# A third row maximum per loop iteration that two heads share, in half-width matmuls, with the loop's transfers on SyncE

## The chip, the cores and the metric

The kernel runs on one core of a Trainium2 chip. Its engines work side by side, each through its own instruction queue in program order: PE (matmuls, and PEld for the weight loads that run ahead of them), DVE (vector work), ACT (activations), POOL (GpSimd) and SP (SyncE, which only issues transfers here). Matmuls write to PSUM, which has 8 banks of 512 float32 for each of 128 partitions. The metric is the device time of one execution in microseconds (us); less is better.

## The reference

The program computes a gated mix of two blocks on the same tokens x (2048 tokens, 640 features). Only block A, attention with 32 heads of width 20, concerns the change:

```python
scores = jnp.einsum("bhqd,bhkd->bhqk", q, k) * (Dh ** -0.5)
p = _softmax(scores, axis=-1)
o = jnp.einsum("bhqk,bhkd->bhqd", p, v)
a = o.transpose(0, 2, 1, 3).reshape(B, S, D) @ wo
```

Block B is a token-mixing MLP (layer norm, two matrices over the token axis, a gelu), and the result is g * a + (1 - g) * b with a sigmoid gate g for each token. Everything is float32.

## The kernel before

**Stages.** First the queries, keys and values are projected (to about 220 us). Then the MLP runs (to about 700 us). Then comes the attention loop (to about 1762 us), and last the output projection. What concerns us is the attention loop, lines 672 to 719.

**Two kinds of score tiles.** Heads are taken in pairs: head j of a pair (j = 0 or 1) keeps its keys and queries in the rows 64 j and up of a 128-row tile, so its matmuls use one half of PE's rows, and a matmul of the other head can run beside it in the other half. A softmax needs the maximum over all keys of each query ahead of the exponentials, so every score is computed twice.

- The *maximum tiles* (line 178, tile `s`): 128 queries against 512 keys of one head, a bank of 128x512 scores; `tensor_reduce` on DVE (line 180) takes the maximum over the 512 keys. A pair of heads has 128 such tiles: two halves of the queries, 8 blocks of 128 queries in each, 4 times 512 keys, 2 heads. After 64 of them `s_max` takes the maximum over the four blocks of keys (line 143, DVE), three small operations on POOL negate it and split it in two parts (lines 144 and 145), and 8 tiles later `s_store` transposes it (line 150, DVE), and it goes to DRAM (line 151). From there `load_m` brings it into two further rows of the queries' tile.
- The *exponential tiles* (line 700, tile `st`): the transposed scores, 128 keys against 512 queries, whose two further rows subtract the maximum; ACT exponentiates each from PSUM into `p` (line 703).

**One iteration.** The loop has 16 pairs times 32 iterations. An iteration takes one block of 128 keys (`kt`) against one half of the queries (`qh`): four exponential tiles (two heads, two times 512 queries), and then, in `pv_flush`, four matmuls side by side in PE's columns that multiply the *previous* iteration's exponentials with the values (line 637, tile `pv`; each shows as two rows in the profile, since plain float32 goes through PE in several passes). After 16 blocks of keys `pv_evac` copies the sums out (line 618, DVE) and stores them with 8 transfers on POOL's queue (lines 624 and 625).

**How the maximum tiles are spread.** 736 of the 2048 maximum tiles (`S_AHEAD`) are computed in the MLP stage. The other 1312 go into the loop, evenly: `due` (line 706) says how many there should be, and `take` of an iteration is 2 or 3 until they are given out, 28 iterations before the end, and then 0. With three, the order on PE is exponential tile, maximum tile, exponential tile, maximum tile, exponential tile, maximum tile, exponential tile. The halves of the rows alternate so that each maximum tile stands beside an exponential tile in the other half; the seventh matmul has nothing beside it. With fewer than three, one exponential tile takes a bank of the maximum tiles (`s_tile` in line 709).

**Banks.** The exponential tiles have four banks in turn (`st_tile`), the maximum tiles three (`s_tile`), and `pv` one. PE must wait for ACT or DVE to have read a bank before it writes there again.

**Queues.** PE's, ACT's and DVE's orders are those of the program; from the MLP on POOL's and SP's are too. On POOL's queue in the loop are the maxima's three operations, the maxima's store, the stores of `pv_evac`, the normalisers' loads and stores (`norm_steps`), and the load and split of the output weights (`load_wo`, with pairs 8 to 12). SP's queue has loads alone: `base_stack` of the next pair (keys and queries for the exponential tiles, 20 transfers, issued at iteration 6), `load_v` (at 12), `s_stack` (keys and queries for the maximum tiles, 18 transfers, at 14), `load_m` (4 transfers, at 27 for the next pair's first half and at 11 for the pair's second half).

Of the kernel before, what the change touches and what calls it, by code (L numbers as in the profile page):

```python
# [13 lines left out]
P = 128  # L14
# [14 lines left out]
def gated_mix(ctx, tc, xT, x, wqk, wv0, wv1, wo, w1, w1t, b1, w2, b2, out):  # L29
# [38 lines left out]
    def st_tile(shape, name):  # L68
        return psum.tile(shape, F32, tag="st", bufs=4, name=name)

    def s_tile(shape, name):
        return psum.tile(shape, F32, tag="s", bufs=3, name=name)

    def k8(shape, dt, name):
        return base.tile(shape, dt, tag="k8", bufs=3, name=name)
# [59 lines left out]
        c0 = NPAIR * (p % 8)  # L135
        nc.sync.dma_start(v_tiles[p], v_d[p // 8, :, :, c0: c0 + NPAIR].rearrange("t p c -> p t c"))

    s_close = []

    def s_max(p, half, mx):  # L140
        mm = cp.tile([P, 16], F32, tag="mm", bufs=2, name=f"mm{p}_{half}")
        mc = cp.tile([P, 32], F32R, tag="mc", bufs=2, name=f"mc{p}_{half}")
        nc.vector.tensor_reduce(mm, mx.rearrange("p k j t -> p (j t) k"), axis=AX.X, op=OP.max)
        nc.gpsimd.tensor_scalar_mul(mm, mm, -1.0)
        hi_lo(mc[:, :16], mc[:, 16:], mm, hi_eng=nc.gpsimd, lo_eng=nc.gpsimd)
        s_close.append([8, lambda: s_store(p, half, mc)])
# [5 lines left out]

    M_LAG = [8]

    def s_next():
        next(stream)()
        for e in list(s_close):
            e[0] -= 1
            if e[0] <= 0:
                s_close.remove(e)  # L160
                e[1]()

    def s_finish():
        next(stream, None)
        while s_close:
            s_close.pop(0)[1]()

    def s_tiles(p):
        for half in range(2):
            mx = cp.tile([P, 4, 2, 8], F32, tag="mx", bufs=2, name=f"mx{p}_{half}")  # L170
            for t in range(8):
                for kc in range(4):
                    for j in (1, 0):
                        def f(j=j, kc=kc, t=t):
                            ks, qs = s_src[p]
                            ps = s_tile([P, 512], f"s{p}_{half}_{t}_{j}_{kc}")
                            r = slice(64 * j, 64 * j + 3 * DH)
                            nc.tensor.matmul(ps, qs[half][r, t * P:(t + 1) * P], ks[r, kc * 512:(kc + 1) * 512],  # L178
                                             start=True, stop=True)
                            nc.vector.tensor_reduce(mx[:, kc, j, t: t + 1], ps, axis=AX.X, op=OP.max)  # L180
                        yield f
            s_close.append([2, lambda p=p, half=half, mx=mx: s_max(p, half, mx)])

    def s_stream(on_start):
        for p in range(NP):
            on_start(p)
            yield from s_tiles(p)

    hooks = [None]
    m_queue = [nc.gpsimd]  # L190
    stream = s_stream(lambda p: hooks[0](p))

    p1s = ExitStack()
    p1 = p1s.enter_context(tc.tile_pool(name="p1", bufs=1, side="right"))
# [353 lines left out]
    for n, _ in enumerate(steps):  # L548
        settle()
        while done + 2 <= S_AHEAD and done < S_AHEAD * (n + 1) / STEPS:  # L550
            if done == 48:
                s_src[1] = base_stack(1, False, None)
            if done == 4 * 128 + 40:
                st_src[0] = base_stack(0, True, None)
                for half in range(2):
                    load_m(0, st_src[0][1], half, lambda *a: drip.append(lambda: nc.sync.dma_start(*a)))
                drip.append(lambda: load_v(0))
            if drip and done % 4 == 0:
                drip.pop(0)()
            for _ in range(2):  # L560
                s_next()
            done += 2
    settle(True)
    while done < S_AHEAD:
        s_next()
        done += 1
    gps.close()
    hps.close()

# [14 lines left out]

    hooks[0] = start_loop
    M_LAG[0] = 0
    s_src[6] = s_stack(6)

    def norm_steps(h0, h1):
        b = (h1 - h0) * S // P  # L590
        a = S // b
        rl = ap.tile([P, 256], F32, tag="rl", bufs=1, name=f"rl{h0}")

        def load():
            nc.gpsimd.dma_start(rl[:, :b], l_d[h0:h1].rearrange("h (a b) -> (h a) b", b=b))

        def recip(i):
            nc.vector.reciprocal(rl[:, i: i + 64], rl[:, i: i + 64])

        def store(h):  # L600
            src = rl[a * (h - h0): a * (h - h0 + 1), :b]
            nc.gpsimd.dma_start(r_d[h].rearrange("d (a b) -> a d b", b=b), src.unsqueeze(1).broadcast_to([a, DH, b]))
# [13 lines left out]
    def pv_evac(p, qh, pv):  # L616
        ev = ap.tile([P, 512], F32, tag="oev", bufs=2, name=f"oev{p}_{qh}")
        nc.vector.tensor_copy(ev, pv)  # L618
        for j in range(2):
            h = 2 * p + j  # L620
            for c in range(2):
                r = 32 * (2 * j + c) + 11 * j
                cols = slice(qh * 1024 + c * 512, qh * 1024 + (c + 1) * 512)
                nc.gpsimd.dma_start(o_d[DH * h: DH * h + DH, cols], ev[r: r + DH, :])  # L624
# [19 lines left out]

    def load_wo(c):
        raw = ap.tile([P, D], F32, tag="wor", bufs=1, name=f"wor{c}")
        nc.gpsimd.dma_start(raw, wo[c * P:(c + 1) * P, :])
# [19 lines left out]
    def o_late(q):  # L667
        return o_part(q, slice((NC - 1) * P, D), 1, 512, "l", 4, nc.scalar, nc.vector)[0]

    turn = given = 0  # L670
    LEFT = NP * 128 - S_AHEAD
    for p in range(NP):
        ks, qs = st_src[p]
# [2 lines left out]
        for it in range(32):  # L676
# [20 lines left out]
            def st_op(j, c, tile):  # L697
                r = slice(64 * j, 64 * j + 3 * DH + 2)
                ps = tile([P, 512], f"st{p}_{it}_{j}{c}")
                nc.tensor.matmul(ps, ks[r, kt * P:(kt + 1) * P], qs[qh][r, c * 512:(c + 1) * 512],  # L700
                                 start=True, stop=True)
                pt = lp.tile([P, 512], F32, tag="pt", bufs=12, name=f"p{p}_{it}_{j}{c}")
                nc.scalar.activation(pt, ps, AF.Exp, scale=SCALE)  # L703
                pts[j, c] = pt

            due = min((p * 32 + it + 1) * LEFT // (NP * 32 - 28) + 1, LEFT)
            take = min(due - given, 3)
            for n in range(4):
                st_op((n + turn) % 2, n // 2, s_tile if n == 2 and take < 3 else st_tile)
                if n < take:  # L710
                    s_next()
            given += take
            if take and given == LEFT:
                s_finish()
            turn = (turn + take) % 2
            pv_flush()
            if p * 32 + it in later:
                later.pop(p * 32 + it)()
# [79 lines left out]
```

## Time and profile before

| | us |
|---|---|
| median of 3 runs (1843.85 to 1847.97) | 1845.69 |
| the profiled execution | 1846.6 |
| its span | 1844.8 |

The profiled execution is one run with the hardware profiler; its own time is 0.9 us over the median, and 1.8 us of it lie outside its span. PE's granted clock was 0.996 of full speed. In the loop (800 to 1700 us) the profile counts 1732 exponentials on ACT and 1175 maxima on DVE.

How to read it: a row of the timeline gives the start, the duration, the engine, the line, and how many instructions were merged. A weight load's start (PEld) marks the moment when PE gets to a matmul; its matmul streams behind it. The duration of a row holds the time to fill and drain the pipeline as well, so rows of one engine overlap, and the distance between starts is the rate. In square brackets stands how long the engine had been idle and what ended that, as far as semaphores tell.

### The profile page before, as it was taken

The page shows a single profiled execution, that of the slowest core. Times are in us where ns is not written, and L with a number is a line of the kernel's source. Part 1 is how long each engine was busy: PE and PEld are TensorE (multiplying, and loading weights), DVE is VectorE, ACT ScalarE, POOL GpSimd, SP SyncE. Part 2 cuts the span into 40 slices and gives each one's busy share as a digit, 9 for nine tenths or more (in the row PEclk, how much of TensorE's full clock was granted, in tenths as well). Part 3 has the DMA queues.
Part 4 walks back from the last instruction along what each step waited for, and adds up shares of the span by engine and source line. Part 5 has one row for each costly group of instructions (what it writes and reads, how often), then busy time and mean ns, then how long its engine had stood idle before and what let it go on. Part 6 is the DMA issues. An engine that isn't in the chain of part 4 may idle for free. (4 is left out here: it accounts for less than half of the span.)

```text
span 1844.8 us, 39129 instructions
## 1 busy us (share of the span) xinstructions
PE 1829.7 (99%) x14978; PEld 1135.2 (62%) x14978; DVE 1428.9 (77%) x2341; ACT 1361.6 (74%) x2688; POOL 637.1 (35%) x900
## 2 busy tenths in 40 slices
PE   9999999999999999999999999999999999999998
PEld 7998799999999994333333333333333333333378
DVE  4202299999999998888888888888888888888137
ACT  4243244465444448999999999999999999999930
POOL 1013478888887770112112111121321211212210
PEclk9999999999999999999999999999999999999999
DMA  8456766566645645504032324213540423301463
GB/s 289 143 169 212 222 173 173 158 194 193 168 139 166 189 136 121 118 15 103 20 85 61 73 42 93 57 50 78 107 103 24 109 47 77 71 14 23 131 219 132
DMA packets 152831, 216.61 MB, mean 117 GB/s; under 512 B 65698, under 2 KB 92082, under 8 KB 148738
## 3 DMA queue, kind: packets, MB, share of 16 engines
q1 hardware_dynamic: 129172, 178.68, 35.4%
q0 software_dynamic: 14688, 20.78, 5.2%
q10 hardware_dynamic: 8784, 14.65, 2.4%
q8 instruction: 118, 1.93, 0.4%
q14 instruction: 69, 0.57, 0.1%
HBM read 165.43 MB, written 48.25 MB: 116 GB/s over the span
## 5 line engine op out<-in xcount | busy, mean ns | idle before, releaser
L180 DVE TENSOR_REDUCE mx<-s 128x1 f32<-128x512 f32 x2048 | 1293.7, 684 | 159.9 <-PE s L178 119.7
L703 ACT ACTIVATE p<-st 128x512 f32<-128x512 f32 x2048 | 1042.1, 615 | 20.9 <-PE s L178 2.2
L700 PEld LDWEIGHTS st<-qs_True,ks_True 62*128 62x128 f32 x2048 | 307.3, 185 | 485.1 <-ACT p L703 312.9
L700 PE MATMUL st<-qs_True,ks_True 62*128 62x512 f32 x2048 | 579.6, 425 | 0.2 <-ACT ty L477 0.2
L637 PE MATMUL pv<-p,v 128*32 128x512 f32 x4096 | 555.5, 605 | 0.2
L178 PE MATMUL s<-sk,sq 60*128 60x512 f32 x1280 | 423.1, 434 | 0.0
L41 POOL TENSOR_TENSOR wl<-wr,wh 128x512 fp32r<-128x512 f32 x228 | 273.6, 1216 | 59.8 <-ACT wh L38 30.9
L624 POOL DMA_DIRECT2D o_d<-oev x128 | 67.0, 524 | 494.3 <-DVE oev L618 491.6
L178 PE MATMUL s<-ks_False,qs_False 60*128 60x512 f32 x768 | 225.1, 397 | 0.4 <-DVE mx L180 0.3
L46 PE MATMUL y<-gh,wh 64*128 64x320 f32 x896 | 216.8, 308 | 0.0
L46 PE MATMUL y<-gl,wh 64*128 64x320 f32 x832 | 210.3, 306 | 0.0
L46 PE MATMUL y<-gh,wl 64*128 64x320 f32 x832 | 209.4, 305 | 0.0
L38 ACT ACTIVATE wh<-wr 128x512 fp32r<-128x512 f32 (+2 forms) x246 | 135.9, 594 | 90.2 <-PE s L178 29.0
L178 PEld LDWEIGHTS s<-sk,sq 60*128 60x128 f32 x1280 | 197.7, 185 | 1.2
L637 PEld LDWEIGHTS pv<-p,v 128*32 128x32 f32 x4096 | 84.9, 108 | 171.4 <-issue 156.4
L46 PE MATMUL u<-hl,wh 64*128 64x320 f32 x864 | 167.1, 306 | 0.0
L46 PE MATMUL u<-hh,wh 64*128 64x320 f32 x864 | 167.1, 306 | 0.0
L46 PE MATMUL u<-hh,wl 64*128 64x320 f32 x800 | 156.9, 306 | 0.4 <-POOL wl L41 0.4
L46 PEld LDWEIGHTS y<-gh,wh 64*128 64x128 f32 x896 | 155.3, 184 | 0.4
L46 PEld LDWEIGHTS y<-gh,wl 64*128 64x128 f32 x832 | 147.0, 184 | 0.3
L46 PEld LDWEIGHTS y<-gl,wh 64*128 64x128 f32 x832 | 146.9, 184 | 0.0
L178 PEld LDWEIGHTS s<-ks_False,qs_False 60*128 60x128 f32 x768 | 124.4, 184 | 1.1 <-DVE mx L180 1.1
(124 smaller groups left out, 1817.6 us busy)
## 6 DMA issues: line engine op xcount, KB each, us to landing
wr<-in_w_dram SPq DMA_DIRECT2D x196, 256.0 KB
ks_True<-k_d SPq DMA_DIRECT2D x96, 160.0 KB
qs_True<-q_d SPq DMA_DIRECT2D x192, 80.0 KB
sk<-k_d SPq DMA_DIRECT2D x60, 160.0 KB
sq<-q_d SPq DMA_DIRECT2D x120, 80.0 KB
v_d<-vt SPq DMA_DIRECT2D x32, 168.0 KB
v<-v_d SPq DMA_DIRECT2D x16, 336.0 KB
xr<-in_xT_dram SPq DMA_DIRECT2D x20, 256.0 KB
```

The costliest lines, as they stand in the source:

```text
L38: nc.scalar.activation(hi, src, AF.Copy)
L41: (lo_eng or nc.vector).tensor_sub(lo, src, hi.bitcast(F32))
L46: nc.tensor.matmul(ps[k], a[r], b[r], start=start, stop=stop)
L178: nc.tensor.matmul(ps, qs[half][r, t * P:(t + 1) * P], ks[r, kc * 512:(kc + 1) * 512], start=True, stop=True)
L180: nc.vector.tensor_reduce(mx[:, kc, j, t: t + 1], ps, axis=AX.X, op=OP.max)
L624: nc.gpsimd.dma_start(o_d[DH * h: DH * h + DH, cols], ev[r: r + DH, :])
L637: nc.tensor.matmul(pv[r: r + 32, :], v_tiles[p][:, kt, 10 * j: 10 * j + 32], pts[j, c], start=(kt == 0), stop=(kt == NT - 1))
L700: nc.tensor.matmul(ps, ks[r, kt * P:(kt + 1) * P], qs[qh][r, c * 512:(c + 1) * 512], start=True, stop=True)
L703: nc.scalar.activation(pt, ps, AF.Exp, scale=SCALE)
```

## The change

In iterations with three maximum tiles, two are of 512 keys, one for each head, as before. The third is now shared: 256 keys of head 0 and the same 256 keys of head 1, side by side in one bank (`s_both`). One reduction takes both maxima, two results of 256 inputs each. The new order on PE for three is: the shared tile's matmul in row half 0 (256 keys), exponential tiles (1,0), maximum tile in half 0, exponential tiles (1,1) and (0,0), maximum tile in half 1, exponential tile (0,1), the shared tile's matmul in half 1 (256 keys). So each half gets three and a half matmuls, shifted against each other by half of one.

The two matmuls of a shared tile write one bank and must not run together. The second therefore waits for a `memset` of one element on POOL (`s_mark`), which waits for the first. There are 344 of these.

A block of queries now has up to 6 partial maxima in place of 4; `mx` is filled with a large negative number on POOL ahead of use (`s_table`), and line 143's reduction takes 6 inputs for each output. The three banks of the maximum tiles are named one by one; the shared tile's bank is held from its first matmul to its second, and goes to the end of the list after the iteration's other two. An iteration with two takes two whole tiles; whether it takes two or three follows `due` as before, and where only 256 keys of a block are left, it takes three.

The maxima's store, the stores of `pv_evac`, the normalisers' transfers and the load of the output weights go from POOL's queue to SP's, but for the last ones behind the end of the loop. The diff, cut to its core:

```diff
-    def s_tile(shape, name):
-        return psum.tile(shape, F32, tag="s", bufs=3, name=name)
+    s_banks, s_held = ["sa", "sb", "sc"], []
+
+    def s_tile(shape, name, hold=False):
+        tag = s_banks.pop(0)
+        (s_held if hold else s_banks).append(tag)
+        return psum.tile(shape, F32, tag=tag, bufs=1, name=name)
...
+    def s_table(i):
+        if i < 2 * NP:
+            s_mx[i] = cp.tile([P, 6, 2, 8], F32, tag="mx", bufs=2, name=f"mx{i}")
+            nc.gpsimd.memset(s_mx[i], -3.0e38)
...
+    def s_mm(ps, piece, j, n):
+        p, half, t, k0 = piece[:4]
+        ks, qs = s_src[p]
+        r = slice(64 * j, 64 * j + 3 * DH)
+        return nc.tensor.matmul(ps, qs[half][r, t * P:(t + 1) * P], ks[r, k0: k0 + n], start=True, stop=True)
+
+    def s_full(piece, j):
+        p, half, t, k0, k, mx = piece
+        ps = s_tile([P, 2 * KB], f"s{p}_{half}_{t}_{j}_{k0}")
+        s_mm(ps, piece, j, 2 * KB)
+        nc.vector.tensor_reduce(mx[:, k, j, t: t + 1], ps, axis=AX.X, op=OP.max)
+        s_tick()
+
+    def s_both(piece):
+        p, half, t, k0, k, mx = piece
+        ps = s_tile([P, 2, KB], f"s{p}_{half}_{t}_x_{k0}", hold=True)
+
+        def part(j):
+            ins = s_mm(ps[:, j], piece, j, KB).ins
+            if j == 0:
+                mark = nc.gpsimd.memset(s_mark, 0.0).ins
+                tc.add_manual_dep(mark, ins.name, sync_dep, reason="first row half done")
+                marks.append(mark)
+            else:
+                tc.add_manual_dep(ins, marks.pop().name, sync_dep, reason="one bank, two row halves")
+                s_banks.append(s_held.pop())
+                nc.vector.tensor_reduce(mx[:, k, :, t], ps, axis=AX.X, op=OP.max)
+                s_tick()
+
+        return part
...
+    m_queue[0] = nc.sync
...
+        put = (nc.gpsimd if qh == 1 and p == NP - 1 else nc.sync).dma_start
...
-                nc.gpsimd.dma_start(o_d[DH * h: DH * h + DH, cols], ev[r: r + DH, :])
-                nc.gpsimd.dma_start(l_d[h: h + 1, cols], ev[r + DH: r + DH + 1, :])
+                put(o_d[DH * h: DH * h + DH, cols], ev[r: r + DH, :])
+                put(l_d[h: h + 1, cols], ev[r + DH: r + DH + 1, :])
...
-            take = min(due - given, 3)
-            for n in range(4):
-                st_op((n + turn) % 2, n // 2, s_tile if n == 2 and take < 3 else st_tile)
-                if n < take:
-                    s_next()
+            want = due - given
+            if want >= 3 and LEFT - given != 4 or want > 0 and s_pos["o"] == 7:
+                first, second = (1, 2) if s_pos["o"] == 7 else (2, 1)
+                a, b = s_take(first), s_take(second)
+                pair, both = (a, b) if first == 2 else (b, a)
+                part = s_both(both)
+                part(0)
+                st_op(1, 0, st_tile)
+                s_full(pair, 0)
+                st_op(1, 1, st_tile)
+                st_op(0, 0, st_tile)
+                s_full(pair, 1)
+                st_op(0, 1, st_tile)
+                part(1)
+                given += 3
+            elif want > 0:
+                pair = s_take(2)
+                st_op(0, 0, st_tile)
+                s_full(pair, 1)
+                st_op(1, 0, st_tile)
+                s_full(pair, 0)
+                st_op(0, 1, s_tile)
+                st_op(1, 1, st_tile)
+                given += 2
```

More of the change, by code (lines that the diff above doesn't have):

```diff
@@ L161, in s_next, with s_ends @@
                 e[1]()
+    def s_ends():
+        while s_over:
+            a = s_over.pop(0)
+            s_close.append([2, lambda a=a: s_max(*a)])
     def s_finish():
-        next(stream, None)
+        s_ends()
         while s_close:
             s_close.pop(0)[1]()
[L168 to L187, printed above, removed]
+    KB = 256
+    s_mark = cp.tile([1, 1], F32, name="s_mark")
+    marks = []
+    sync_dep = mybir.DependencyInfo(mybir.DependencyClass.Sync, mybir.DependencyReason.DATA)
+    s_mx = {}
+    def s_table(i):
+        if i < 2 * NP:
+            s_mx[i] = cp.tile([P, 6, 2, 8], F32, tag="mx", bufs=2, name=f"mx{i}")
+            nc.gpsimd.memset(s_mx[i], -3.0e38)
+    s_pos = {"t": 0, "o": 0, "k": 0}
@@ L559, in gated_mix @@
                 drip.pop(0)()
-            for _ in range(2):
-                s_next()
+            s_pair()
             done += 2
@@ L706, in gated_mix @@
             due = min((p * 32 + it + 1) * LEFT // (NP * 32 - 28) + 1, LEFT)
[L707 to L713 removed]
+            want = due - given
[22 more added lines that the diff above has]
+                given += 2
+            else:
+                for n in range(4):
+                    st_op(n % 2, n // 2, s_tile if n == 2 else st_tile)
+            if s_over and given == LEFT:
                 s_finish()
[L715 removed]
+            s_ends()
             pv_flush()
```

43 lines of the change are left out of this document (33 added, 10 removed).

## The prediction

> **What bounds the kernel now.** I read the page first (span, engines, costliest groups), then the windows of the attention loop, then single iterations in the timeline of PE, PEld, DVE and POOL.
>
> ```profile
> span 1844.8 us, 39129 instructions
> PE 1829.7 (99%) x14978; PEld 1135.2 (62%) x14978; DVE 1428.9 (77%) x2341; ACT 1361.6 (74%) x2688; POOL 637.1 (35%) x900
> ...
> L180 DVE TENSOR_REDUCE mx<-s 128x1 f32<-128x512 f32 x2048 | 1293.7, 684 | 159.9 <-PE s L178 119.7
> L703 ACT ACTIVATE p<-st 128x512 f32<-128x512 f32 x2048 | 1042.1, 615 | 20.9 <-PE s L178 2.2
> ```
> ```profile
> 900.00:1000.00 100.00, 100.00 (x710) 38.55 (x707) 84.41 (x138) 98.05 (x194) 14.66 (x32) 1.00 0.32 74
> ...
> 1700.00:1750.00 50.00, 49.88 (x318) 15.46 (x312) 12.18 (x18) 49.85 (x103) 16.14 (x24) 1.00 0.36 113
> ```
>
> The columns of the windows are PE, PEld, DVE, ACT, POOL, clock, DMA. In 100 us of the loop ACT does 194 exponentials, 48.5 iterations of four, so an iteration lasts 2.06 us. ACT looks full at 98.05, but its rows overlap. At the end, where no maxima are left, it does 103 in 49.85, 0.484 each, so four take 1.94 us. ACT is 0.12 us per iteration from being the bound, DVE is at 84%, and PE is at work all the time. PE's order of work is therefore the first suspect. The weight loads that open each section show it:
>
> ```profile
> 1081.23 0.18 PEld L700 LDWEIGHTS st<-qs_True,ks_True 62*128 62x128 f32 x1 [0.84 <-ACT p L703]
> ...
> 1083.13 0.18 PEld L700 LDWEIGHTS st<-qs_True,ks_True 62*128 62x128 f32 x1 [0.84 <-issue]
> ...
> 1083.88 0.18 PEld L700 LDWEIGHTS st<-qs_True,ks_True 62*128 62x128 f32 x1 [0.20 <-ACT p L703]
> ...
> 1085.31 0.18 PEld L700 LDWEIGHTS st<-qs_True,ks_True 62*128 62x128 f32 x1 [0.84 <-ACT p L703]
> ...
> 1087.44 0.18 PEld L700 LDWEIGHTS st<-qs_True,ks_True 62*128 62x128 f32 x1 [0.84 <-ACT p L703]
> ...
> 1089.34 0.18 PEld L700 LDWEIGHTS st<-qs_True,ks_True 62*128 62x128 f32 x1 [0.84 <-issue]
> ```
>
> An iteration with two maximum tiles (a "two") lasts 1.90 (1081.23 to 1083.13, and 1087.44 to 1089.34). The first three behind it lasts 2.18, the next three 2.13. The first three is longer because its last exponential tile waits for ACT (1083.88): a two puts only three tiles into the four banks, so the next iteration soon needs the bank that the two's last exponential still reads. So **a two and the three behind it last 4.08 together, set by ACT**, and a three behind a three is PE's own:
>
> ```profile
> 1064.37 0.49 PE L700 MATMUL st<-qs_True,ks_True 62*128 62x512 f32 x1
> ...
> 1064.71 0.62 PE L700 MATMUL st<-qs_True,ks_True 62*128 62x512 f32 x2
> 1064.95 0.39 PE L178 MATMUL s<-sk,sq 60*128 60x512 f32 x1
> 1065.18 0.40 PE L700 MATMUL st<-qs_True,ks_True 62*128 62x512 f32 x1
> 1065.51 1.07 PE L637 MATMUL pv<-p,v 128*32 128x512 f32 x8
> 1066.51 0.49 PE L700 MATMUL st<-qs_True,ks_True 62*128 62x512 f32 x1
> ```
>
> Four slots: starts 0.34, 0.24, 0.23 apart, 0.33 to the values' matmuls, and 1.00 for those. A slot is 0.235; the first has 0.10 more, its weights, so its matmuls begin at 0.10. How many threes are there? 1312 tiles in 512 - 28 = 484 iterations make 344 threes and 140 twos. So 140 threes stand first behind a two, and 204 behind a three.
>
> **What the new order can win.** Do the halves run apart, and what does half a matmul cost? The MLP shows it, with 320 columns in one half beside 512 in the other:
>
> ```profile
> 690.28 0.31 PE L46 MATMUL y<-gh,wh 64*128 64x320 f32 x1
> 690.29 0.39 PE L178 MATMUL s<-ks_False,qs_False 60*128 60x512 f32 x1
> 690.42 0.30 PE L46 MATMUL y<-gl,wh 64*128 64x320 f32 x1
> 690.52 0.30 PE L46 MATMUL y<-gh,wl 64*128 64x320 f32 x1
> 690.57 0.39 PE L178 MATMUL s<-ks_False,qs_False 60*128 60x512 f32 x1
> ```
>
> One half starts at 0.28, 0.42, 0.57 (0.145 for 320 columns), the other at 0.29 and 0.52 (0.23 for 512): they don't wait for each other, and the time goes with the columns, so 256 take 0.117. The Trainium skill (TensorEngine Tiling, Instruction Overhead) gives each matmul about 60 cycles besides its columns; by that 320 columns would take 0.155 of the measured 0.145, so the trace doesn't agree, and by it the sum would be some 2 us higher. The longer half's work falls from 4 slots to 3.5, and an undisturbed three from 2.13 to 2.01. The 140 first threes hang on ACT and win nothing. That leaves 204 x 0.117 = 24 us.
>
> **What the banks take back.** Three banks serve the maxima, and DVE reads them at its own pace:
>
> ```profile
> 1064.94 1.89 DVE L180 TENSOR_REDUCE mx<-s 128x1 f32<-128x512 f32 x3 [0.24 <-PE s L178]
> ```
>
> Three reductions start 0.605 apart ((1.89 - 0.68) / 2); the first starts 0.57 behind the section's start, so 0.47 behind its matmul's. Now: 0.57 + 1.21 + 0.68 = 2.46 until the third bank is read, and 0.05 for the word to reach PE (between 0 and the 0.10 that POOL shows below). The third maximum of the next iteration loads its weights at 2.13 + 0.47, so there are 0.09 to spare. After: the first whole maximum starts at 0.10 + 0.117, and its reduction 0.45 later (between 0.39, the length of the row at 1064.95, and 0.47), at 0.67. The shared tile is read last, to 0.67 + 1.21 + 0.68 = 2.56, with the word 2.61. Its bank is the one that the next three needs for its second whole maximum, and the next two for its third exponential tile, both with weights at 0.47. So **an iteration and the wait in the next add up to at least 2.61 - 0.47 = 2.14**: behind a short three of 2.01 the next waits 0.13. Followed through two, three, three: first three 2.18, second 2.01, two 1.90 + 0.13 = 2.03, first three 4.08 - 2.03 = 2.05, second 2.01 + 0.09 = 2.10, two 1.94, first three 2.14, second 2.01, and so on. The second threes average 2.055, 0.075 under now: 140 x 0.075 = 10.5. The 64 further threes win 0.03: 2. **Of 24 us, 12.5 remain.**
>
> **What the rest costs.** First come timeline rows of DVE and POOL at one merging of maxima, then groups (count | busy us, mean ns | idle us before):
>
> ```profile
> 1413.60 0.25 DVE L143 TENSOR_REDUCE mm<-mx 128x16 f32<-128x64 f32 x1
> ...
> 1413.95 0.25 POOL L144 TENSOR_SCALAR mm<-mm 128x16 f32<-128x16 f32 x1 [4.80 <-DVE mm L143]
> 1414.27 0.20 POOL L40 CAST mc<-mm 128x16 fp32r<-128x16 f32 x1
> 1414.55 0.23 POOL L41 TENSOR_TENSOR mc<-mm,mc 128x16 fp32r<-128x16 f32 x1
> ...
> L311 POOL MEMSET vt<- 128x16 f32 x32 | 4.0, 132 | 112.8 <-DMA v_d<-vt 88.5 <-DMA k_d<-evl 24.3
> L85 POOL MEMSET eps_t<- 128x1 f32 x1 | 0.1, 89 | 0.0
> ...
> L41 POOL TENSOR_TENSOR wol<-wor,woh 128x640 fp32r<-128x640 f32 x5 | 7.8, 1554 | 0.4
> L40 POOL CAST woh<-wor 128x640 fp32r<-128x640 f32 x5 | 3.6, 715 | 17.2 <-DMA wor<-in_wo_dram 17.2
> ...
> L618 DVE COPY oev<-pv 128x512 f32<-128x512 f32 x32 | 21.9, 683 | 39.9 <-PE pv L637 39.9
> ```
>
> *The mark.* The shared tile's first matmul starts at 0.10, streams 0.117 and is reported 0.20 later, at 0.42; POOL starts 0.10 later (1413.85 to 1413.95), the memset takes 0.09 to 0.13, and PE hears of it 0.05 later: 0.66 to 0.70. Wanted are the weights at 0.70 (matmul at 0.10 + 3 x 0.235, weights 0.10 ahead). Behind the waiting matmul stand the values' matmuls and so all of PE. I take no cost; there is hardly any slack.
>
> *The merged maxima*, 21 times in the loop (1312 / 64). DVE's step of 0.25, some 0.03 longer with six inputs for four, stands ahead of the shared tile's reduction and makes the bank 0.2 later; today 0.09 of that is slack, so 0.1 more. POOL's three operations end 0.93 behind DVE's (1414.78), and the next mark queues behind them: about 3.2 behind the section's start, where the next three, waiting for its bank too, wants it at 2.9 to 3.1; two times in three the next is a three: 0.15. 21 x 0.25 = +5.
>
> *The output weights*, 5 times: cast and subtraction hold POOL 2.3, from 0.65 to 2.95, and the next mark could start at 2.01 + 0.52: 0.45 late. +2.
>
> *The copies of* `pv_evac`, 31 in the loop: 0.6 more on DVE makes the next reductions 0.43 late where they are 0.29 late now; half of them count: 31 x 0.07 = +2.
>
> *Fillings and lengths:* a fill of `mx` (96 columns, between 0.13 and the cast's 0.7) falls once in 24 iterations on an idle POOL: nothing, and at most 0.2 x 21 = 4 without that cover.
>
> *SyncE* (its timeline, a row of the queue's waits with sum, times and longest, and a group of POOL's):
>
> ```profile
> 934.59 0.46 SPq L105 DMA_DIRECT2D ks_True<-k_d  x1
> ...
> 945.94 0.34 SPq L115 DMA_DIRECT2D qs_True<-q_d  x1
> 948.19 2.72 SPq L129 DMA_DIRECT2D qs_True<-m_d  x4
> ...
> SPq L136 <- PE s L178: 322.8, 10, 48.1
> L624 POOL DMA_DIRECT2D o_d<-oev x128 | 67.0, 524 | 494.3 <-DVE oev L618 491.6
> ```
>
> SP runs up to 48 us ahead today. Behind stores that wait for DVE it can't: a pair's 20 loads go out when the previous pair's sums are stored, at about iteration 2. They take 11.7 us, six iterations; the maxima's rows follow, 2.7 us, by about iteration 11, wanted at 16. Per pair SP is at work some 37 of 66 us (11.7, about as much for the 18 loads, 2 x 2.7, and 16 stores at POOL's 0.52). I take nothing: five iterations, 10 us, cover it. POOL loses its 0.52 us issues, but was idle 494 us ahead of them: nothing won.
>
> **Sum.** -12.5 + 5 + 2 + 2 = -3.5, less the hardly covered mark, put at +1.5: **-2 us**. From the profiled execution's 1846.6 (span 1844.8) that is 1844.6; it lies 0.9 over the median, so against the median 1843.7: **1844**, no difference that can be measured (0.2%, 3.7 us, is about what a measurement can tell).
>
> **Rivals.**
> - *The mark comes late* (slower). POOL's answer decides from 0.70 on. One that is 0.1 late costs 0.1 on 344 threes, less the 0.05 of bank wait that it replaces on average: +17, 1861; each further 0.1 costs 34. For it: the sum is on the edge, and no row shows POOL waiting for PE. Against: the memset's rows are short. 0.18.
> - *The banks don't bite*: DVE frees the shared bank 0.1 earlier. Then 24 less 4 for POOL: 1824. Against: reductions of 0.605 are steady. 0.10.
> - *SP's order bites*: rows of maxima 1 us late once in each of 16 pairs: +16, 1860. For it: loads and stores in one order. 0.12.
> - *The change doesn't do what it says*: the half matmul takes a whole slot. Nothing is won and the costs remain, with later reductions: +9 to +20, 1860. Against: the MLP's rows. 0.08.
>
> **How the numbers follow.** The forecast has 0.52 and its own range 1838 to 1850 (the wait of 0.13 by 0.03 either way changes 204 threes by 6): 0.18 of it faster, 0.27 within 0.2%, 0.07 slower. With the rivals: faster 0.28, same 0.30 (with the mildest of SP's cases), slower 0.42. The range 1828 to 1868 leaves out most of the early banks and the marks over 0.1 late.
>
> **What would show it.** In the profile after: threes behind threes alternating about 2.0 and 2.1; twos up to 2.03; waits on DVE `mx` ahead of the second whole maximum; a mark's memset about 0.1 long that ends under 0.7 behind the section's start. PE waiting for POOL in plain threes, or matmuls of the halves starting together, would prove it wrong; so would waits for loads at the start of a pair.

## The result, and the profile after

| | us (median, range, runs) | ratio to the kernel before, 95% interval |
|---|---|---|
| before | 1844.88 (1843.85 to 1847.97, 4) | |
| after | 1856.49 (1854.24 to 1859.17, 4) | 1.0061 [1.0042, 1.0079] |

The change makes the kernel slower by 0.6%, 11.6 us. The profiled execution of after took 1854.24, 1852.5 of it span. It is the fastest of the four, and that of before (1846.6) lies 1.7 over its median, so the two profiles differ by 7.7 us of span and not by 11.6. First the page of after (engines with busy time, share and instructions; groups with count, busy us, mean ns, and the idle time ahead of them):

```profile
span 1852.5 us, 40514 instructions
...
PE 1827.3 (99%) x15322; PEld 1150.9 (62%) x15322; DVE 1432.9 (77%) x2341; ACT 1360.5 (73%) x2688; POOL 510.6 (28%) x971
...
L219 DVE TENSOR_REDUCE mx<-s 128x1 f32<-128x512 f32 x1704 | 1087.3, 685 | 157.7 <-PE s L213 129.8
L761 ACT ACTIVATE p<-st 128x512 f32<-128x512 f32 x2048 | 1040.9, 616 | 27.3 <-PE st L758 15.1
...
L229 POOL MEMSET s_mark<- 1x1 f32 x344 | 30.3, 88 | 896.9 <-PE st L758 869.4
```

PE's busy time fell by 2.4 us while the span grew by 7.7, and ACT's idle time ahead of its exponentials grew from 20.9 to 27.3: PE itself waits somewhere. The windows (PE, PEld, DVE, ACT, POOL, granted clock, DMA share, GB/s) say where it doesn't, and where it does:

```profile
900.00:1000.00 100.00, 99.92 (x751) 40.30 (x748) 85.02 (x140) 98.63 (x195) 4.69 (x43) 1.00 0.35 74
...
1325.00:1330.00 5.00, 5.00 (x42) 1.95 (x36) 4.02 (x7) 5.00 (x11) 0.30 (x3) 1.00 0.47 70
1330.00:1335.00 5.00, 1.98 (x16) 0.69 (x16) 2.21 (x4) 2.42 (x5) 0.09 (x1) 0.90 0.36 45
1335.00:1338.00 3.00, 2.35 (x10) 1.05 (x14) 1.38 (x2) 1.35 (x3) 0.00 (x0) 0.50 0.71 129
1338.00:1341.00 3.00, 3.00 (x16) 1.35 (x8) 1.18 (x2) 1.47 (x4) 0.09 (x1) 0.53 0.58 113
```

In a quiet stretch after does 195 exponentials in 100 us where before did 194: a quiet stretch of the loop is no slower. But from 1332 to 1341 PE stands still for 3 us and then runs at half its clock.

**A quiet stretch** is just what the prediction drew. The weight loads that open the sections:

```profile
1080.19 0.18 PEld L758 LDWEIGHTS st<-qs_True,ks_True 62*128 62x128 f32 x1 [0.84 <-ACT p L761]
...
1080.70 0.19 PEld L758 LDWEIGHTS st<-qs_True,ks_True 62*128 62x128 f32 x2 [0.22 <-DVE mx L235]
...
1082.13 0.18 PEld L213 LDWEIGHTS s_x<-sk,sq 60*128 60x128 f32 x1 [0.84 <-DVE mx L219]
...
1084.26 0.18 PEld L213 LDWEIGHTS s_x<-sk,sq 60*128 60x128 f32 x1 [0.84 <-DVE mx L219]
...
1086.28 0.18 PEld L758 LDWEIGHTS st<-qs_True,ks_True 62*128 62x128 f32 x1 [0.84 <-ACT p L761]
...
1086.86 0.19 PEld L758 LDWEIGHTS st<-qs_True,ks_True 62*128 62x128 f32 x2 [0.29 <-DVE mx L235]
...
1088.30 0.18 PEld L213 LDWEIGHTS s_x<-sk,sq 60*128 60x128 f32 x1 [0.84 <-DVE mx L219]
...
1090.35 0.18 PEld L213 LDWEIGHTS s_x<-sk,sq 60*128 60x128 f32 x1 [0.84 <-DVE mx L219]
```

A two of 1.94, a first three of 2.13, a second of 2.02, a two of 2.02, a first three of 2.05, a second of 2.05: the prediction's list had 1.94, 2.14, 2.01, 2.03, 2.05, 2.10. In both twos the third section's weights wait for the reading of the shared bank (L235). Medians over the iterations of the loop, measured between such rows (a later three is the third in a row; after has 8 fourth ones besides):

| | two | first three | second three | later threes |
|---|---|---|---|---|
| before | 1.896 | 2.176 | 2.129 | 2.129 |
| after | 1.991 | 2.108 | 2.055 | 2.113 |

**Where the time went.** Thirteen iterations of after last over 2.4 us; together they stand 14.3 us above the medians of their kinds. Before has one, 0.5 above. Most of the sum lies in two pairs of heads: pair 9's iterations 0, 8 and 15 to 17, and pair 10's 0 and 1, 12.1 us (iteration 8's 0.4 of it stands in every kernel here with the shared tile). These are the pairs beside which the first normaliser runs: 16 stores (`r_d`, 160 KB each) that start in pair 8 and end in pair 9. Its effect is seen in SyncE's timeline (start, duration, issues):

```profile
1304.04 3.29 SPq L659 DMA_DIRECT2D r_d<-rl  x3
1307.37 2.84 SPq L109 DMA_DIRECT2D ks_True<-k_d  x1
...
1323.43 0.27 SPq L119 DMA_DIRECT2D qs_True<-q_d  x1
1324.34 0.66 SPq L659 DMA_DIRECT2D r_d<-rl  x2
1325.42 2.19 SPq L155 DMA_DIRECT2D m_d<-mt  x1
1327.65 2.71 SPq L659 DMA_DIRECT2D r_d<-rl  x1
1330.41 4.47 SPq L133 DMA_DIRECT2D qs_True<-m_d  x4
...
1356.42 8.01 SPq L659 DMA_DIRECT2D r_d<-rl  x5
1364.48 4.53 SPq L133 DMA_DIRECT2D qs_True<-m_d  x4
1369.11 0.40 SPq L705 DMA_DIRECT2D wor<-in_wo_dram  x1
```

The 20 loads of a stack take 16 us here (1307.4 to 1323.7) against the forecast's 11.7; two sorts of stores stand between them and the rows of maxima (`qs_True<-m_d`), which are issued at 1330.4 to 1334.9, when PE wants them at 1332. Summed over its rows, SyncE issues for 51.9 us in the 73.1 us that this pair lasts (47 in its first 66), and for 16 to 23 in each of pairs 1 to 7. There the rows of maxima for a pair's second half are out 3 to 11 us ahead of the iteration that reads them, in pair 9 only 0.2. PE and POOL at the two worst places:

```profile
1330.91 1.07 PE L695 MATMUL pv<-p,v 128*32 128x512 f32 x8
1335.07 0.76 PE L758 MATMUL st<-qs_True,ks_True 62*128 62x512 f32 x1 [3.09 <-DMA qs_True<-m_d]
...
1337.60 1.94 PE L695 MATMUL pv<-p,v 128*32 128x512 f32 x8
...
1371.41 0.41 PE L758 MATMUL st<-qs_True,ks_True 62*128 62x512 f32 x1
1374.59 0.38 PE L213 MATMUL s_x<-sk,sq 60*128 60x256 f32 x1 [2.77 <-POOL s_mark L229]
...
1370.86 0.26 POOL L148 TENSOR_SCALAR mm<-mm 128x16 f32<-128x16 f32 x1 [3.64 <-DVE mm L147]
...
1371.47 0.23 POOL L41 TENSOR_TENSOR mc<-mm,mc 128x16 fp32r<-128x16 f32 x1
1372.18 0.72 POOL L40 CAST woh<-wor 128x640 fp32r<-128x640 f32 x1 [0.49 <-DMA wor<-in_wo_dram]
1372.98 1.53 POOL L41 TENSOR_TENSOR wol<-wor,woh 128x640 fp32r<-128x640 f32 x1
1374.45 0.09 POOL L229 MEMSET s_mark<- 1x1 f32 x1
```

At 1332 PE waits 3.09 for rows of maxima. At 1371 it waits 2.77 for a mark: ahead of the mark POOL has the merging of the maxima (0.84), a wait of 0.49 for the output weights, which SyncE issued late, and their conversion (2.3). After both waits PE runs at half speed for a while (the values' matmuls take 1.94 and 1.93, not 1.07). So the wait of 3.09 made three iterations 6.0 us longer than their medians, and that of 2.77 two iterations 4.6.

**The theories.** A: the forecast's loop is right, and the loss comes from what is queued in order behind the normaliser's stores on SyncE, and behind the weights' conversion on POOL. B: small costs of the mark and the maxima everywhere, of which the profile's stalls are only an accident. Others came up on the way.

### The profile page after: what moved, and what is told of

Read it like the earlier page. It is cut to its first block, busy times and chain, and to the rows that moved or that the text cites. A ratio compares the mean times of both kernels' runs of the same rounds, so it can differ in the third digit from the quotient of the medians.

```text
span 1852.5 us, 40514 instructions
## 1 busy us (share of the span) xinstructions
PE 1827.3 (99%) x15322; PEld 1150.9 (62%) x15322; DVE 1432.9 (77%) x2341; ACT 1360.5 (73%) x2688; POOL 510.6 (28%) x971
## 5 line engine op out<-in xcount | busy, mean ns | idle before, releaser
L219 DVE TENSOR_REDUCE mx<-s 128x1 f32<-128x512 f32 x1704 | 1087.3, 685 | 157.7 <-PE s L213 129.8
L761 ACT ACTIVATE p<-st 128x512 f32<-128x512 f32 x2048 | 1040.9, 616 | 27.3 <-PE st L758 15.1
L758 PEld LDWEIGHTS st<-qs_True,ks_True 62*128 62x128 f32 x2048 | 282.2, 185 | 200.6 <-ACT p L761 129.2
L213 PE MATMUL s<-sk,sq 60*128 60x512 f32 x944 | 361.8, 421 | 0.0
L213 PEld LDWEIGHTS s_x<-sk,sq 60*128 60x128 f32 x672 | 123.6, 184 | 290.5 <-DVE mx L219 269.0
L229 POOL MEMSET s_mark<- 1x1 f32 x344 | 30.3, 88 | 896.9 <-PE st L758 869.4
L235 DVE TENSOR_REDUCE mx<-s_x 128x2 f32<-128x512 f32 x344 | 234.4, 681 | 3.2 <-PE s_x L213 3.2
L213 PE MATMUL s_x<-sk,sq 60*128 60x256 f32 x672 | 225.6, 336 | 3.5 <-POOL s_mark L229 3.5
L46 PE MATMUL u<-hl,wh 64*128 64x320 f32 x864 | 193.0, 306 | 0.0
L46 PE MATMUL u<-hh,wh 64*128 64x320 f32 x864 | 192.6, 305 | 0.0
L213 PEld LDWEIGHTS s<-sk,sq 60*128 60x128 f32 x944 | 165.2, 186 | 21.3 <-DVE mx L235 11.7
```

Source lines behind the costliest of these rows:

```text
L46: nc.tensor.matmul(ps[k], a[r], b[r], start=start, stop=stop)
L213: return nc.tensor.matmul(ps, qs[half][r, t * P:(t + 1) * P], ks[r, k0: k0 + n], start=True, stop=True)
L219: nc.vector.tensor_reduce(mx[:, k, j, t: t + 1], ps, axis=AX.X, op=OP.max)
L229: mark = nc.gpsimd.memset(s_mark, 0.0).ins
L235: nc.vector.tensor_reduce(mx[:, k, :, t], ps, axis=AX.X, op=OP.max)
```

## Experiments

All times are medians; ratios are to the kernel before, run beside each on the same chip. Not all runs were made beside each other, and the medians of before lie between 1843.84 and 1845.80. Where two runs with different runs of before are compared and the ratios give another size, both are given.

**1. The rows of maxima earlier** (`rows_early`)

```diff
                 if it == 27:
                     load_m(p + 1, st_src[p + 1][1], 0)
+                    if p + 1 <= 12:
+                        load_m(p + 1, st_src[p + 1][1], 1)
-            if it == 11 and p:
+            if it == 11 and p > 12:
```

> Against the change: for pairs up to 12 the second half's rows of maxima are loaded at iteration 27 of the pair before, right behind the first half's, and no longer at iteration 11. Theory A (SyncE's one order: in pairs 9 and 10 the normaliser's 16 stores stand ahead of loads that PE and POOL wait for; two stalls of 6.0 and 4.6 us and one of 1.05 make up the whole loss): the stall of 6.0 us at pair 9, iterations 15 to 17, goes and the one at pair 10 stays, 1850.5. Theory B (the mark and the maxima's merging cost a little in every iteration, and the stalls of the one profiled execution are not typical): within 1.5 us of the change, 1855 to 1858.

1859.49, ratio 1.0085 [1.0066, 1.0103]: a miss for both, 3 us slower than the change. The stall in pair 9's iteration 15 is gone as expected. But the four more loads stand ahead of the output weights, and those stand ahead of the marks: pair 9 starts with 7.0 and 3.3 us, pair 10 with 14.6. In the waits of this kernel from 1370 to 1390:

```profile
POOL woh L40 <- DMA wor<-in_wo_dram: 8.8, 1, 8.8
...
PEld s_x L213 <- POOL s_mark L229: 5.6, 1, 5.6
```

Whatever comes last in SyncE's order is late there; to exchange two loads only moves the stall.

**2. The weights' conversion later** (`wo_split`)

```diff
-        hi_lo(woh[c], wol[c], raw, hi_eng=nc.gpsimd, lo_eng=nc.gpsimd)
+        wo_raw[c + 8] = (woh[c], wol[c], raw)
...
+            if it == 13 and p in wo_raw:
+                hi_lo(*wo_raw.pop(p), hi_eng=nc.gpsimd, lo_eng=nc.gpsimd)
```

> Against the change: the output weights are loaded as before, and POOL converts them 13 iterations later, so that no mark stands behind a conversion that still waits for its load. Theory A: the stalls at the first iteration of pairs 9 and 10 go (1.05 and 4.6 us), but for some 0.45 each by which a conversion of 2.3 us holds up a mark; the stall for rows of maxima stays: 1851.5. Theory B: within 1.5 us of the change, 1855 to 1858.

1851.09, ratio 1.0033 [1.0020, 1.0046]: 5.4 us less than the change, as theory A has it. Both stalls at the start of pairs 9 and 10 are gone from the profile, the one in pair 9 at iteration 15 is still there (6.0 us of an iteration).

**3. Both** (`rows_wo`)

> Both edits together (rows of the second half early, conversion of the output weights late), all transfers still on SyncE. Theory A: everything that the normaliser's stores made late is gone, and what is left is the prediction's sum without SyncE: 1843 to 1846, no iteration over 2.7 us in the loop. Theory B: 1852 or more. In between: other loads are late too.

1852.08, ratio 1.0037 [1.0024, 1.0050]: a miss. Pair 10 now begins with an iteration of 8.3 us. SyncE's timeline of this kernel:

```profile
1353.78 8.01 SPq L659 DMA_DIRECT2D r_d<-rl  x5
1361.83 7.28 SPq L133 DMA_DIRECT2D qs_True<-m_d  x8
```

Five of the normaliser's stores take 8 us to issue, and behind them stand the rows that PE wants at 1363. So theory A's place was right, but moving the loads that suffer doesn't cure it.

**4. The queue without the shared tile** (`queue_only`): the kernel before with the same transfers on SyncE.

```diff
+    m_queue[0] = nc.sync
...
+        put = (nc.gpsimd if h1 == H else nc.sync).dma_start
...
-        nc.gpsimd.dma_start(raw, wo[c * P:(c + 1) * P, :])
+        nc.sync.dma_start(raw, wo[c * P:(c + 1) * P, :])
```

> The kernel before with the loop's transfers moved to SyncE as in the change, without the shared tile. Theory A, with the stall for the rows of maxima in PE's way whatever the tiles are: 1849 to 1852, and a gap of some 3 us of PE in pair 9. Conversions that come late hold up no mark here, so no stall at pair 10. Theory C (it takes the shared tile and the marks for the queue to matter): 1845, as before.

1853.58, ratio 1.0047 [1.0032, 1.0063]. The new queue alone costs 9 us, without a shared tile or a mark. So theory C falls, and theory B can't explain the larger part of the loss. The profile has the one gap that A named, in its waits:

```profile
PE st L704 <- DMA qs_True<-m_d: 3.7, 1, 3.7
```

Its two iterations stand 5.2 us above their medians. This profiled execution took 1851.38, the shortest of the four, so the rest of the 9 us is not seen in it.

**5. The normalisers back on POOL** (`norm_pool`: the change; `queue_less`: number 4)

```diff
-        put = (nc.gpsimd if h1 == H else nc.sync).dma_start
+        put = nc.gpsimd.dma_start
```

> Against the change: the normalisers' loads and their 28 stores in the loop stay on POOL's queue as before; all else is on SyncE. Theory A' (in the change SyncE's issues fill 47 us of the 66 of pair 9 against 16 to 23 in pairs without a normaliser, because the normaliser's stores of 160 KB take up to 2.7 us each to issue; loads behind them are late, of rows and of weights): SyncE falls back to 25 us or less in pair 9, no iteration over 2.7 us, 1843 to 1846. POOL's issues, 0.64 each, follow a mark and end before the next: no cost. Theory D (the order of the sums' and maxima's stores costs too): 1848 to 1852.

> The kernel before with all of the loop's transfers on SyncE except the normalisers': no shared tile. Theory A': 1845, as before, against 1853.6 with the normalisers' on SyncE too. Theory D: 1848 to 1852. Its distance to norm_pool is what the shared tile is worth by itself: -2 by the prediction's sum.

`queue_less`: 1845.44, ratio 1.0005 [0.9996, 1.0014]. All the rest of the new queue costs nothing that can be measured, and the normalisers' transfers (their loads and 28 stores) cost the 8 us between the two. `norm_pool`: 1850.97, ratio 1.0031 [1.0021, 1.0042], 5.5 less than the change but 5 more than the most that was expected. No load of maxima is late any more (the rows of pair 9's second half are out 5.4 us ahead). What I had wrong: SyncE still issues for 41.9 us in pair 9, not 25, since its other issues take up to 2.7 there too, even with the stores on POOL. And pair 10 still begins with 5.2 us, with the weights in time. POOL's timeline of `norm_pool`:

```profile
1363.62 0.26 POOL L148 TENSOR_SCALAR mm<-mm 128x16 f32<-128x16 f32 x1 [3.65 <-DVE mm L147]
1363.94 0.20 POOL L40 CAST mc<-mm 128x16 fp32r<-128x16 f32 x1
1364.23 0.23 POOL L41 TENSOR_TENSOR mc<-mm,mc 128x16 fp32r<-128x16 f32 x1
1364.40 0.72 POOL L40 CAST woh<-wor 128x640 fp32r<-128x640 f32 x1
1365.19 1.53 POOL L41 TENSOR_TENSOR wol<-wor,woh 128x640 fp32r<-128x640 f32 x1
1366.67 0.09 POOL L229 MEMSET s_mark<- 1x1 f32 x1
```

The merging and the conversion meet in one iteration, and one mark waits for both.

**6. Both of these** (`norm_wo`: `wo_split` with the normalisers on POOL)

> norm_pool with the conversions of the output weights 13 iterations behind their loads. Theory A': in norm_pool the weights land in time already, so 1843 to 1846 here too, within 2 us of norm_pool; if weights still land late there, this one is 2 to 6 us faster.

1847.78, ratio 1.0013 [1.0004, 1.0023]: 3.2 less than `norm_pool`, more than the 2 expected. The iterations of 5.2 and 3.0 us at the start of pair 10 are gone from the profile, so this was the meeting just shown and not late weights.

**7. The shared tile alone** (`tile_only`): the change with all of the loop's transfers on POOL, as before.

> The shared tile with all of the loop's transfers on POOL as in the kernel before. Each pair's 16 stores of sums (0.52 each) hold up about eight marks by up to 8.3 us in all in the iteration after a pair's half, twice per pair; the mark queues behind them. By the prediction's figures 31 halves cost some 4 us each less 1.3 of slack, 80 to 120 us: 1930 to 1960. If the stores find their place between marks, 1845.

2052.14, ratio 1.1122 [1.1100, 1.1144]; the expectation's direction was right, and its size half of what came. Its waits:

```profile
PEld s_x L213 <- POOL s_mark L229: 135.5, 44, 7.3
...
PE s_x L213 <- POOL s_mark L229: 110.6, 29, 7.0
```

Behind 30 of the 32 `pv_evac` a mark stands behind eight stores, and PE behind the mark, up to 7.3 us. PE's gaps there add up to some 135 us, not far from the expected 80 to 120. The clock adds to that: PE's granted clock was 0.953 over this run, 0.995 in after, which makes up to some 85 us more (an estimate: 0.042 of 2050 us; part of it falls into the gaps). This is what the move to SyncE is for: the shared tile can't live beside stores on POOL's queue.

**8. The mark's edge** (`mark_twice`) **and the banks** (`x_half_read`), both on `norm_wo`

```diff
                 tc.add_manual_dep(mark, ins.name, sync_dep, reason="first row half done")
+                mark = nc.gpsimd.memset(s_mark, 0.0).ins
```
```diff
-                nc.vector.tensor_reduce(mx[:, k, :, t], ps, axis=AX.X, op=OP.max)
+                nc.vector.tensor_reduce(mx[:, k, :, t], ps[:, :, :KB // 2], axis=AX.X, op=OP.max)
```

> norm_wo (1847.8) with a second write to the mark's tile behind the first, and the second half matmul waits for that one: POOL's answer comes later by one operation, 0.09 busy and at most 0.1 more. By the prediction POOL's answer stands at its edge: 0.1 late on 344 threes less the 0.05 of bank wait that it replaces, 17 us: 1865; 0.15 late: 1880. Rival: the answer has 0.1 to 0.2 to spare because the threes wait for banks anyway: within 3 us of norm_wo.

> norm_wo with the shared tile's maxima read from the first 128 of the 256 keys in either row half: the maxima over the other 128 are left out, and DVE's third step of an iteration takes some 0.42 instead of 0.68. By the prediction the shared bank sets the iterations (2.14 for an iteration and the wait in the next), and with this bank free 0.26 sooner the wait is gone: second threes 2.01 instead of 2.06, twos 1.90 instead of 1.99, 10 to 13 us in all, 1835 to 1838. Rival: the mark or the order of the halves sets them; then no change, 1846 to 1849.

`mark_twice`: 1858.86, ratio 1.0077 [1.0062, 1.0093], 11.1 more than `norm_wo`. `x_half_read`: 1837.16, ratio 0.9958 [0.9942, 0.9974], 10.6 less, inside what was expected. The shared tile's group in it:

```profile
L235 DVE TENSOR_REDUCE mx<-s_x x344: 381/417/426, 703.9 to 1692.5; 128x2 f32<-128x256 f32 x172
```

Medians of the iterations:

| | two | first three | second three | later threes |
|---|---|---|---|---|
| norm_wo | 1.988 | 2.106 | 2.057 | 2.110 |
| mark_twice | 1.923 | 2.153 | 2.102 | 2.102 |
| x_half_read | 1.893 | 2.186 | 2.015 | 2.063 |

With the bank free 0.26 sooner the twos, first and second threes come within 0.01 of the forecast's undisturbed 1.90, 2.18 and 2.01. With one memset more, threes behind threes have the same length in every place, 2.10, 0.09 over 2.01: the mark now sets them, and it had no slack.

**9. The normaliser thinner, on SyncE** (`norm_sparse`: `wo_split` with four iterations between its steps, not two)

```diff
-                later[at if n == 0 else at + 10 + 2 * n] = f
+                later[at if n == 0 else at + 10 + 4 * n] = f
```

> wo_split (normalisers on SyncE, 1851.1) with the normaliser's steps four iterations apart instead of two, so that its 16 stores lie over two pairs and a bit. If the sum of SyncE's work in pair 9 is what makes loads late (47 of 66 us issuing, the rest waiting), it falls to some 35 in two pairs, the rows come in time, and this comes to norm_wo's 1846 to 1848. If one long issue ahead of a load is enough, however few there are: 1850 or more.

1845.11, ratio 1.0010 [1.0001, 1.0020], 6.0 less than `wo_split` (4.2 by the ratios), by one number in one line. SyncE issues for 37.4 us in pair 9 and 28.3 in pair 10 (51.7 and 17.7 in `wo_split`), and the rows of maxima for pair 9's second half and pair 10's first are out 5.5 and 8.6 us ahead. Eleven issues between 1304 and 1437 us still take over 1.5 us. So it is the crowd of stores in one pair, not a single long issue.

**10. The normaliser's loads on SyncE, its stores on POOL and later** (`norm_both`)

> norm_wo with the normalisers' loads on SyncE, where the sums that they read are stored too, and their stores still on POOL but two to four iterations later, so that no store waits on POOL for DVE's reciprocals: in norm_wo a load that waited for the stores held a mark up 1.8 us in pair 12 and a store 0.8 in pair 14. Theory: those 2.6 us go, 1845, no difference to the kernel before. If other things make norm_wo slower than before: 1847.8.

1847.42, ratio 1.0015 [1.0006, 1.0025]. The two stalls of 1.8 and 0.8 us are gone from its profile, and its loop is 2.1 shorter than `norm_wo`'s, but the time is only 0.4 less, so the runs don't tell the two apart.

**11. The MLP** (`mlp_lean`). In its profile the loop of `norm_sparse` was 4.6 us shorter than that of before (1051.0 against 1055.6, from the end of iteration 1), and yet its time was no shorter. In the profiles the loop starts late. Weight loads of the exponential tiles (the first time is the start of the first one), in before and in `norm_sparse`:

```profile
L700 PEld LDWEIGHTS st<-qs_True,ks_True x2048: 182/186/331, 698.1 to 1759.7; 62*128 62x128 f32 x187
```
```profile
L761 PEld LDWEIGHTS st<-qs_True,ks_True x2048: 182/183/189, 700.8 to 1757.3; 62*128 62x128 f32 x187
```

From the MLP's first matmul to its last pass 472.8 to 473.2 us in the three profiles with the old stream of maxima, and 474.1 to 477.6 in the eleven with the new one. DVE and POOL in `norm_wo`:

```profile
227.75 2.48 DVE L219 TENSOR_REDUCE mx<-s 128x1 f32<-128x512 f32 x4 [1.29 <-POOL mx L185]
...
226.33 1.27 POOL L41 TENSOR_TENSOR wtmp<-wr,wtmp 128x512 fp32r<-128x512 f32 x1 [1.44 <-ACT wtmp L38]
227.53 0.19 POOL L185 MEMSET mx<- 128x96 f32 x1
```

The first table's fill queues on POOL, and DVE, which has no time to lose in the MLP, waits for it. PE waits in turn: near 227 us it stands still for 1.55 us in after, 1.74 in `norm_wo` and 3.36 in `norm_sparse`, and for no gap over 0.6 in before and in `mlp_lean`.

```diff
-            nc.gpsimd.memset(s_mx[i], -3.0e38)
+            if i > 10:
+                nc.gpsimd.memset(s_mx[i], -3.0e38)
...
-        nc.vector.tensor_reduce(mm, mx.rearrange("p k j t -> p (j t) k"), axis=AX.X, op=OP.max)
+        nc.vector.tensor_reduce(mm, mx[:, :4 if 2 * p + half < 11 else 6].rearrange("p k j t -> p (j t) k"), axis=AX.X, op=OP.max)
```

> norm_sparse (1845.1) in which the eleven tables of maxima that the MLP fills alone are not filled by POOL beforehand and are merged over the four pieces that they have, not six; the loop is as it was. Theory E (the change also made the MLP dearer, which the prediction did not price: 474 to 478 us from its first to its last matmul in the profiles with the new stream against 473 with the old one; DVE waited 1.29 for the first fill behind POOL's conversions, and eleven merges take 0.06 more each): the MLP falls by 2 us and the whole to 1843, within 0.1% of the kernel before. Rival: the MLP's difference comes from its order of instructions, not from fills and merges; then 1845, and the MLP stays at 475 or more.

1843.39, ratio 0.9988 [0.9979, 0.9996]. The MLP takes 472.6 and the loop's first exponential tile starts at 697.9, so the 2 to 3 us were the fills and merges (the two edits were not run one by one). This is the fastest of all that computes the whole result: the change with three small edits, 0.12% faster than before.

## Why the prediction was wrong, point by point

The forecast was 1844, no change; measured are 1856.5 and slower. What the forecast said of the iterations themselves held, but for some 5 us; most of the loss lies in terms that it put at nothing or too low. The rival *SP's order bites*, with a chance of 0.12, named the larger part of the cause.

- **The failed step is *SyncE***: "I take nothing: five iterations, 10 us, cover it." The 37 of 66 us were counted for a pair without a normaliser, with the issue times of a quiet stretch. Quiet pairs in after take less, 16 to 23, but have 3 to 11 us of cover and not 10. Pair 9 has up to 16 more stores, and beside them other issues get longer too: SyncE was at work for 51.9 us. The rows of maxima came out when PE wanted them, not five iterations ahead. The queue alone costs 9 us (`queue_only`). Taking the stores off SyncE wins 5.5 us (`norm_pool`), 8.1 without the shared tile (`queue_less` against `queue_only`), and spreading them 6.0 (`norm_sparse` against `wo_split`; 4.2 by the ratios). The rival had the kind right and the form wrong: not 1 us in each of 16 pairs, but 3 in one, doubled to 6 with the half clock behind it. The trace of before had a sign of it: while its pair 9 ran and the normaliser's stores stood on POOL, the four loads that took 2.72 in the forecast's stretch took much longer; everywhere else in its loop they took 2.7 to 3.6:

```profile
1325.29 6.49 SPq L129 DMA_DIRECT2D qs_True<-m_d  x4
...
1347.29 4.69 SPq L129 DMA_DIRECT2D qs_True<-m_d  x4
```

- ***The output weights*, 5 times 0.45, +2: too small.** It is 5.4 (`wo_split`), from two of five conversions. A mark behind a conversion with no merging beside it made an iteration 1.08 longer in pair 9 (there too POOL waited 0.87 for the weights); where conversion and merging meet, and the weights land late too, 4.6. The step put every cost beside an otherwise idle POOL and never let two meet.
- **The MLP wasn't in the sum.** The fills and the wider merging were costed where POOL is idle, in the loop; in the MLP POOL is at 81% and DVE at 99% (300 to 400 us in before). That cost 2 to 3 us in the profiles; between `norm_sparse` and `mlp_lean` it is 1.7 by the medians and 4.1 by the ratios.
- ***What the new order can win* was right.** The half matmul takes 0.12 (1084.27 to 1084.49 in half 0, less 0.10 for the section's first weights). The rival of a whole slot is dead.
- ***What the banks take back* was right**, in mechanism and size: `x_half_read` gives back 10.6 where 24 less 12.5 were said to be lost, 11.5. By the table of medians the second threes win 10.3 us (forecast 10.5) and the later ones 1.0 (2). But a two and its first three together last 4.10 where before's last 4.07, which loses 3.8 that the forecast had at nothing: 7.5 of its 12.5 are left.
- ***The mark* was right at the edge.** In the three at 1084.26 it is written from 1084.77 to 1084.86 and the second half's weights load at 1084.91, 0.65 behind the start; 0.66 to 0.70 was forecast. `mark_twice` prices 0.09 more at 11.1 us, where the rival had 17 for 0.1. By the medians the first and second threes lose 0.05 each, as the rival had it, 13 us; later threes lose nothing, and the twos get back 0.065 each of their bank wait, 9 us, which wasn't allowed for. The iterations above their medians add 6.6 us more than in `norm_wo` and bring the sum to some 10.
- ***Merged maxima and copies***: the iterations of the loop stand above their medians by 6.3 us in all in `norm_sparse` and by 2.8 in before: 3.5, where 7 stood. No run takes these two apart.
- **A slip in a rival**: *The banks don't bite* takes its 20 us off the forecast's 1844; off the 1845.7 of before they give 1826.

Put together from the runs: the loop by itself wins some 4.6 in the profile of `norm_sparse` (forecast without the conversions: 4), the conversions lose 5.4 (of which 2 was forecast), the queue 4 to 6, and the MLP 2 to 3. That is some 7 to 9 of the 11.6 us, and each of these differences is sure to 1 or 2 us; the rest is open. The two profiles themselves close better: by the medians of the table after's iterations win 7.5 us, those above their medians lose 13.3, and the loop is 5.8 longer; 1.6 of the 7.7 us of span lie ahead of it. At the other end the sum closes: `mlp_lean`'s loop is 3.0 shorter than that of before in the profiles, and its time by its ratio 2.2.

What stays open: why issues on SyncE take up to 2.8 us while the normaliser's stores run. They do so with the stores on POOL's queue too (`norm_pool`: SyncE at work for 41.9 us in pair 9), but not always: in `queue_less`, where POOL issues the same stores in short bursts, it is 26.4 us. No run takes the stores' transfers away altogether.

## What to carry to other kernels

When transfers go to a queue that had loads alone, add up its issues in the fullest stretch, not the usual one, with the issue times that the trace shows in that stretch, and look for what is queued behind each store. A wait on a side engine that sits on the main engine's path turns everything else on that side engine into a cost, and two of those can meet. A half-used slot is only won as far as the buffers come free in time: price the last reader's bank before the matmul.

## What the runs showed of the hardware

PE's clock falls after short gaps. After 3.09 us without a matmul the granted clock was 0.50 and 0.53 for the next 6 us (the windows above), after 2.77 it was 0.50 from 1375.1 to 1378.3. After 2.21 us (`norm_pool`, pair 10) it was 0.50 from 1367.6 to 1370.9, and after 1.74 (`norm_wo`, at the first fill) 0.50 from 229.6 to 232.8. After 1.5 us (a late mark in pair 12 of `norm_wo`) it stayed at 1.00. The Trainium skill (TensorE: Matmul & The Clock Gate, Part 1) gives an idle window of about 3.4 us as what sets the array to half its clock; the half clock is what these traces show, but the gaps that were enough are shorter than that window.

The issue of one `r_d<-rl` store on SyncE takes 0.27 us at the least, 0.46 in the median and up to 2.84. Of the 15 issues of the loop of after that take over 1.5 us, 13 lie between 1284 and 1367, while the first normaliser runs, on loads and stores alike. In this kernel a price per issue from a quiet stretch was too low for a full one.
